# DeltaNet and a multiplicative FFN on one core: outputs without a drain, narrower corner products, and a new list of steps

## The chip, the core and the metric

The kernel runs on one core of a Trainium2 chip. A core has five engines that run side by side, each through its own queue in order: TensorE (PE, with its weight loads, PEld), VectorE (DVE), ScalarE (ACT), GpSimd (POOL), and SyncE (SP), which here only issues DMAs. TensorE multiplies a stationary block by a moving one and writes to PSUM; DVE and ACT read PSUM, POOL does not. The metric is the device time of one execution, in microseconds (us); lower is better.

## What is computed

The reference is a delta-rule attention followed by a feed-forward block. Batch 4, 8 heads, 768 tokens, head size 48; the FFN has 3072 tokens, model width 384, hidden width 1024; all in fp32.

```python
for t in range(S):
    kt, vt, bt = (k_n[:, :, t], v[:, :, t], beta[:, :, t, None])
    y[:, :, t] = np.einsum('bhd,bhde->bhe', q[:, :, t], state)
    v_old = np.einsum('bhde,bhd->bhe', state, kt)
    state = state + bt[:, :, :, None] * np.einsum('bhd,bhe->bhde', kt, vt - v_old)
...
a = x @ w1
b = x @ w2
h = a * b @ w3
return h @ w_out
```

Here `k_n` is k with each row divided by its norm, and `x` is y with the heads of a token put side by side.

## The kernel before

**Tiling.** The 768 tokens are cut into 12 chunks of 64 (`C`), and chunks are taken two at a time (`j = m // 2`), which makes 512 token rows of the FFN (`u`). A tile holds two batches (z = 0, 1) in its two halves of 64 partitions, two more (r = 0, 1) and the 8 heads along the free side. `half(z)` is partitions 64z to 64z+63, `feat(z)` the first 48 of them, `quarter(x)` partitions 32x to 32x+31.

**Steps.** Each piece of work is a Python generator that issues some instructions and yields. A list of names, `ORDER` (line 39), says in which sequence all the steps are taken; the n-th time a name stands there, the n-th step of that piece is issued. At the end `in_text_order` ties every engine's instructions to the sequence of the list. So the list sets the order in each of the five queues, and the semaphores set who waits for whom. The pieces, with m a chunk, j a pair, u an FFN block:

- `k`, `q`, `v`, `p`: loads by SP (`p` is eight DMAs a step). `P`: a piece of a weight: loads by SP into one of five `raw` buffers (four DMAs for `P24` to `P35`), two passes on ACT, two on DVE, and an add on POOL that frees the buffer.
- `d`, `K`, `Q`: k and q turned to features first. `g`, `N`, `n`: norms and scaling (`g` has squares on POOL in an `o` buffer, sums on DVE).
- `s` (`scores`, line 371): for each r, TensorE forms K·K and K·Q of all heads in a pair of PSUM banks; DVE writes `U`; then ACT copies the K·Q part to `PT` (line 405) and POOL masks it (chunks 0, 1 and 4 to 11), or DVE does both (chunks 2 and 3).
- `u`, `V`, `e`: a triangular inverse of 64x64 blocks, by 32x32 blocks. `V` is 31 pairs of small DVE instructions for two chunks; in PSUM, it holds one of the two pairs of banks meanwhile. `e` (`corner`, line 543) makes the off-diagonal corner: a 32x32 transpose on DVE (line 557), two rounds of TensorE products (line 574), with copies by ACT after each (lines 605 and 622). For pairs 0 and 1 (`TURNED`, chunks 0 to 3) the blocks are turned by copies instead of a trip through DRAM.
- `c` (`chain`): the state's chain from chunk to chunk: a product with the state, a subtraction on DVE, the product with the inverse, `X` on DVE (line 688), the product for the new state, and its sum on DVE.
- `y` (`outputs`, line 714): below. Its `xT` is the FFN's input; six small DMAs (line 779) then spread each head's last 16 features.
- `t`, `f`: W3·W_out folded. `a0`, `b` (line 872): the first FFN block. `a`, `h`, `i`, `j` (line 991): the others, by a scheme of fewer products; `G`, `W`, `S`, `T` form its sums on POOL. `o` (line 1101) and `x`: the last product and the stores, through two `o` buffers.

**PSUM.** Eight banks of 512 fp32 columns: `two_banks()` hands out two pairs in turn (`ps_w`), to scores, corners, chain, outputs and the inverse; `bank()` hands out four single ones (`ps_f`) to the rest.

**Outputs before.** For each head h and batch half z there is a state product (48 rows, from `feat(h % 2)`) and an X·PT product (64 rows, from half (z + h) % 2), which add up in PSUM. The place is `feat(h // 4)` and bank (h + z) % 2. X·PT of a bank thus comes from one half of the rows, while the state products come from the head's own half: for z = 0 the two agree, for z = 1 they don't. So all products of the first sort are issued, then TensorE is drained (`pe.drain()`), then the state products of z = 1 are issued:

```python
        for mode, todo in enumerate(modes):
            if mode:
                drain = pe.drain().ins
```

TensorE's counts in the profile are twice those of the code: each fp32 product shows as two matmuls (32 products in the code are 64 in a row of the profile).

Of the kernel before, what the change touches and what calls it, by code (L numbers as in the profile page):

```python
# [39 lines left out]
V0 P0 k0 beta P18 P13 P0 P18 P0 P0 P11 g0 P13 K0 P18 K0 P11 P18 P10 P13 P13 q0 P3 P3 P11 g0 beta  # L40
beta K0 K0 K0 k1 K1 P10 P11 P12 P3 P12 g0 g0 Q0 P10 g0 g0 g0 g0 g0 P8 Q0 Q0 Q0 K1 K1 K1 Q0 K1 P3
N0 P9 k2 P8 P8 P10 s0 P8 N0 g1 s0 s0 s0 s0 s0 s0 u0 q1 P2 Q1 P9 p2 P2 P12 P12 P9 Q1 g1 Q1 Q1 P2
u0 g1 Q1 d2 d2 u0 P5 P1 t0 t0 t5 t5 P9 t2 t2 P4 P6 s1 s1 P5 P5 P2 s1 P1 s1 s1 s1 u1 g1 P1 u1 u1
t4 V0 V0 P5 V0 V0 P4 t10 P7 P4 t3 t3 V0 V0 P1 f1 P6 P6 t4 V0 P7 V0 V0 t10 t1 P14 P7 P4 V0 f0 V0
P6 P16 P16 V0 V0 P7 t1 s0 P19 P19 P19 P19 V0 f1 P17 k3 p2 v1 V0 V0 P14 P14 P14 V0 f2 P17 f2 f0 V0
f2 P15 v0 P20 f1 t11 f0 P17 P17 f5 V0 V0 P16 t11 P16 t8 P15 V1 V0 t8 f5 t9 V0 V0 t6 P15 V0 n0 n0
f5 V0 V0 V0 V0 t9 P20 P20 V0 t6 P22 P22 P22 f4 P23 P23 V0 f4 f4 P21 P21 P15 t7 t7 V0 s1 V0 V0 V0
V0 g1 d2 d2 P22 f3 f3 P24 P20 g1 g1 p3 g1 P26 p3 P30 e0 e0 e0 t12 t14 e1 e1 g1 f3 e0 e0 d3 d3 N1
s2 s2 s2 P23 P23 t12 e0 f6 e0 p4 s2 P24 e1 e1 t14 s2 e0 P24 s2 P25 c0 P26 f7 u2 P30 P24 c0 e1 e1
P21 P21 d3 d3 y0 y0 P26 P26 P31 t15 t13 s3 s3 s3 s3 s3 s3 t13 c0 n1 n1 P32 t15 u2 u2 u3 c0 P30 f7  # L50
e1 P25 P25 P31 P31 P27 c1 c1 u3 u3 f6 e1 c1 V1 V1 V1 y0 P31 f6 f7 P25 P27 V1 V1 V1 V1 P30 b1 c1
# [5 lines left out]
d5 p5 c2 c2 y2 a04 e3 s4 N2 e3 s4 a03 s4 b6 b6 s4 s4 s4 s4 T e3 T T d5 n3 d5 a04 e3 b4 b4 b7 s5
n3 k6 g3 u4 s5 s5 s5 s5 s5 s5 b5 b7 b5 a05 T c3 c3 a06 a05 a06 u5 V2 p6 g3 a07 a07 c3 c3 g3 S0 S0
S0 V2 g3 V2 V2 N2 oD0 y3 y3 V2 V2 W oA0 S0 S0 V2 V2 S0 S0 S0 c3 v5 n5 V2 V2 S0 S0 S0 S0 V2 v4 oB0
V2 V2 V2 xA0 V2 V2 xB0 V2 V2 oA0 S0 S0 S0 n4 oB0 xA0 d6 y3 k7 xA0 V2 n4 oC0 V2 V2 V2 a10 xB0 S0  # L60
V2 V2 xC0 G1 V2 xD0 a10 a10 V2 oC0 a10 a10 d6 xC0 xC0 xC0 xD0 V2 V2 i10 V2 h10 c3 c4 V2 V2 j10 V2
V2 V2 a10 h10 i10 a12 V2 V2 h10 W W a12 p6 V2 a12 a12 j12 e4 g3 g3 h10 c4 a12 h10 a12 h12 d6 d6
# [6 lines left out]
V3 V3 V3 V3 a20 a20 i20 h20 a22 h20 g4 c5 g4 g4 g4 a22 V3 j22 d8 h20 h20 e6 i20 g4 a22 d8 a22 h22
a22 a22 i22 e6 V4 e6 c6 i20 h22 e6 i22 h22 n7 h22 e6 e6 a21 a21 a21 n6 c6 p9 c6 s8 i22 N4 h21 h22  # L70
i21 a21 s8 a21 s6 c6 y6 s8 s8 j21 s8 v8 a21 h21 i21 y6 d9 d9 e7 p9 e7 s8 s8 e7 e7 s7 h21 h21 i21
h21 a23 c6 c6 e7 a23 i23 a23 n8 n8 d9 e7 S2 N4 d9 a23 s9 s9 s9 s9 s9 n7 s9 k10 s9 u8 g5 a23 a23
c7 c7 h23 h23 i23 i23 c7 c7 g5 u9 h23 h23 V4 V4 V4 j23 h23 S2 g5 g5 V4 V4 V4 V4 p10 v9 V4 y7 y7
V4 V4 oA2 V4 V4 d10 V4 y7 V4 V4 S2 oD2 S2 d10 xA2 V4 S2 S2 oB2 oC2 V4 c7 xB2 V4 V4 V4 V4 oB2 xB2
xC2 xD2 p10 V4 V4 V4 oA2 V4 V4 a30 a30 G3 a30 a30 S2 S2 oC2 k11 V4 xC2 j30 s9 V4 xD2 xC2 V4 V4 V4
V4 V4 V4 xA2 xA2 xC2 g5 a30 h30 a30 i30 a32 h30 V4 V4 V4 e8 h30 i30 c7 a32 j32 h30 h30 g5 a32 a32
i32 g5 g5 d10 d10 i30 a32 a32 e8 h32 h32 i32 p11 e8 e8 a31 a31 c8 e8 s8 c8 g5 a31 j31 e8 c8 n9 c8
h32 h32 h32 y8 y8 c8 e9 e9 i31 d11 d11 h31 e9 e9 n9 a31 c8 s10 a31 p11 i32 N5 s10 s10 a31 h31 s10
s10 s10 s10 c9 c9 h31 e9 e9 d11 d11 u10 i31 i31 s11 a33 a33 S3 a33 v11 h31 h31 s11 s11 s11 s11
s11 a33 c9 i33 a33 a33 c9 h33 h33 s11 u11 i33 i33 j33 h33 h33 V5 V5 V5 V5 y9 S3 h33 V5 V5 V5 v10  # L80
n10 n10 oA3 S3 S3 V5 V5 oD3 V5 oB3 s10 y9 y9 oC3 V5 V5 S3 S3 V5 V5 V5 V5 V5 xA3 xB3 V5 V5 n11 V5
V5 oB3 V5 xB3 xD3 xC3 xC3 xD3 oA3 G4 a40 S3 S3 a40 a40 V5 oC3 N5 V5 V5 V5 xA3 a40 a40 xC3 h40 a40
h40 i40 V5 V5 V5 V5 h40 h40 V5 j40 h40 i40 V5 V5 V5 V5 a42 a42 a42 a42 i42 h42 a42 j42 xA3 V5 V5
a42 i40 h42 i42 h42 h42 a41 a41 a41 a41 h41 a41 V5 e10 e10 e10 e10 h42 n11 a41 i42 h41 i41 i41
i41 h41 e10 e11 h41 e10 c9 j41 a43 a43 a43 S4 c9 e11 e11 e11 h41 c10 c10 h43 c10 a43 e11 j43 xC3
a43 c10 a43 i43 h43 i43 i43 h43 h43 e11 h43 c10 c10 y10 y10 c11 s11 oD4 c11 c11 c11 oA4 xA4 y11
S4 S4 S4 oB4 oA4 y11 y11 S4 S4 S4 xA4 xB4 oB4 xB4 oC4 xC4 xA4 a50 xC4 S4 oC4 xC4 xD4 xD4 a50 G5
a50 h50 a50 a50 i50 a50 h50 i50 i50 h50 h50 j50 h50 a52 a52 a52 a52 i52 a52 a52 h52 a51 h52 i52
j52 h52 h52 h52 i51 a51 a51 a51 h51 i52 S5 a51 a51 h51 i51 j51 h51 h51 i51 a53 a53 a53 a53 h53
a53 a53 h53 j53 h51 h53 h53 h53 i53 i53 i53 xC4 o5 x5 o5 S5 S5 o5 o5 x5 S5 S5 S5 S5 o5 x5 x5 o5  # L90
x5 x5 x5 x5 x5 x5 S5 o5 x5 x5 x5 x5
# [1199 lines left out]
```

## Time and profile before

| | |
|---|---|
| time, median of 3 runs | 556.02 us (555.83 to 556.4) |
| time of the profiled execution | 556.05 us |
| its span, first to last instruction | 554.0 us |
| granted TensorE clock, mean | 0.997 |
| scores, TensorE, K·K and K·Q at once (line 381) | x384, mean 287 ns |
| scores, TensorE, 64 columns (line 387) | x768, mean 228 ns |
| outputs, X·PT (line 747) | x768, mean 216 ns |
| outputs, state (line 747) | x704, mean 221 ns |
| xT copies, ACT, 48x256 (line 768) | x96, mean 366 ns, 30.5 us in all |
| mask, POOL, 128x512 (line 407) | x20, mean 1285 ns |
| X, DVE, 128x768 (line 688) | x12, mean 953 ns |

The page gives each engine's busy time in 40 slices of the span (13.85 us each); a digit is tenths, 9 is 90% or more:

```profile
PE   3577999999999999999999999999999999999997
PEld 2464666688788988889988889988899888998897
DVE  4989998899877878659977579858587654123332
ACT  4788388855543112332022530123231121300000
POOL 8575554633658970455343355510492212342141
PEclk9998999999999999999999999999999999999999
```

Matmuls overlap one another, so a row's mean duration is longer than what one costs in a run; the distance from the start of one group to the start of the next says what a group takes. In a row of a group, the last columns are busy time, mean duration, and idle time of the engine just before, with what ended it. In a row of the timeline they are start and duration in us, engine, line, operation, tiles, shape and count, and in brackets the idle time before and what ended it.

### The profile page before, as it was taken

What the parts mean: (1) busy time and instruction counts of PE and PEld (TensorE: products, weight loads), DVE (VectorE), ACT (ScalarE), POOL (GpSimd) and SP (SyncE); (2) the same over time, 40 slices, a digit from 0 to 9 for tenths busy, and PEclk for the clock granted to TensorE, in tenths of its full rate; (3) what the DMA queues carried; (4) which work ended last, traced back from release to release, by engine and by line L of the source; (5) the groups of instructions that cost most, each with busy time, mean ns of one, the idle gap of its engine ahead of it and who ended that gap; (6) DMA issues with size and microseconds to landing.
All of it is one profiled execution on the core that took longest, in us unless ns stands there. A gap on an engine that the chain in (4) does not pass through costs nothing.

```text
span 554.0 us, 19883 instructions
## 1 busy us (share of the span) xinstructions
PE 522.9 (94%) x8540; PEld 448.4 (81%) x8540; DVE 389.2 (70%) x850; ACT 188.4 (34%) x393; POOL 257.7 (47%) x278
## 2 busy tenths in 40 slices
PE   3577999999999999999999999999999999999997
PEld 2464666688788988889988889988899888998897
DVE  4989998899877878659977579858587654123332
ACT  4788388855543112332022530123231121300000
POOL 8575554633658970455343355510492212342141
PEclk9998999999999999999999999999999999999999
DMA  8976986579457345345553564253601220020001
GB/s 254 213 199 193 208 184 134 130 154 142 61 82 128 74 110 86 57 96 92 100 109 63 80 121 85 83 81 46 124 15 44 62 52 2 10 66 1 0 1 57
DMA packets 197687, 52.64 MB, mean 95 GB/s; under 512 B 185344, under 2 KB 191488, under 8 KB 197600
## 3 DMA queue, kind: packets, MB, share of 16 engines
q1 hardware_dynamic: 193408, 50.59, 44.8%
q10 hardware_dynamic: 4192, 0.79, 1.0%
q8 instruction: 67, 1.10, 0.8%
q14 instruction: 20, 0.16, 0.1%
HBM read 41.25 MB, written 8.91 MB: 91 GB/s over the span
## 4 chain that ended last, share of the span: by engine, by line
PE 77%; DVE 6%; ACT 6%; DMA 5%; SPq 3%; issue 1%; POOL 1%; ACTq 0%; POOLq 0%; DVEq 0%
PE ps_f L991 33%; PE ps_f L1101 19%; PE ps_f L872 7%; PE ps_w L648 5%; PE ps_w L747 4%; PE ps_w L574 3%; PE ps_w L387 2%; PE ps_w L381 2%; DMA raw<-in_moe_w_dram 1%; DMA ktok<-in_k_dram 1%; SPq L251 1%; ACT columns L444 1%; DVE w L804 1%; ACT KQ L360 1%; DVE tb L482 1%
## 5 line engine op out<-in xcount | busy, mean ns | idle before, releaser
L999 DVE TENSOR_TENSOR ab<-ab,ps_f 128x512 f32<-128x512 f32 x80 | 54.6, 683 | 58.4 <-PE ps_f L991 57.8
L1072 POOL TENSOR_TENSOR ab<-ab 128x512 f32<-128x512 f32 (+1 forms) x56 | 61.3, 1119 | 42.7 <-PE ps_f L1101 25.9
L991 PE MATMUL ps_f<-xT,w1s 128*128 128x256 f32 x320 | 78.5, 382 | 0.0
L1038 POOL TENSOR_TENSOR ab<-ab,late 128x512 f32<-128x512 f32 x19 | 24.1, 1271 | 107.8 <-DVE ab L999 106.3
L991 PEld LDWEIGHTS ps_f<-xT,w1s 128*128 128x128 f32 x320 | 59.9, 190 | 7.9
L1101 PE MATMUL ps_f<-w,ab 128*128 128x192 f32 x376 | 65.5, 328 | 0.0
L1101 PEld LDWEIGHTS ps_f<-w,ab 128*128 128x128 f32 x376 | 61.3, 190 | 1.3 <-issue 0.7
L852 PE MATMUL ps_f<-w2s,w3T 128*128 128x384 f32 x128 | 45.3, 505 | 4.9 <-POOL w2s L808 4.9
L407 POOL TENSOR_TENSOR PT<-PT,smask 128x512 f32<-128x512 f32 x20 | 25.7, 1285 | 50.8 <-ACT PT L405 50.8
L1101 PE MATMUL ps_f<-room,ab 128*128 128x192 f32 x272 | 47.2, 328 | 0.0
L498 DVE TENSOR_TENSOR ps_w<-ps_w,tb 128x31 f32<-128x31 f32 (+15 forms) x124 | 43.3, 349 | 4.2
L768 ACT COPY xT<-ps_w 48x256 f32<-48x256 f32 x96 | 30.5, 366 | 44.5 <-PE ps_w L747 44.0
L1101 PEld LDWEIGHTS ps_f<-room,ab 128*128 128x128 f32 x272 | 44.3, 190 | 0.6 <-issue 0.3
L493 DVE TENSOR_TENSOR tb<-ps_w,Ub 128x31 f32<-128x31 f32 (+15 forms) x124 | 42.0, 338 | 3.6 <-ACT ps_w L473 0.3
L1007 ACT COPY ab<-ps_f 128x512 f32<-128x512 f32 x20 | 11.7, 586 | 95.0 <-PE ps_f L991 89.3
L991 PE MATMUL ps_f<-xT,room 128*128 128x256 f32 x160 | 41.3, 385 | 0.2 <-DVE ab L999 0.2
L852 PEld LDWEIGHTS ps_f<-w2s,w3T 128*128 128x128 f32 x128 | 24.0, 195 | 20.5 <-POOL w2s L808 5.5
L991 PE MATMUL ps_f<-xT,w2s 128*128 128x256 f32 x160 | 40.1, 381 | 0.0
L991 PE MATMUL ps_f<-x_room,w2s 128*128 128x256 f32 x160 | 38.9, 386 | 0.0
L991 PEld LDWEIGHTS ps_f<-xT,room 128*128 128x128 f32 x160 | 29.5, 190 | 5.4 <-DVE ab L999 1.0
L991 PEld LDWEIGHTS ps_f<-x_room,w2s 128*128 128x128 f32 x160 | 29.5, 190 | 5.2 <-DVE late L999 1.0
L808 POOL TENSOR_TENSOR w<-w,raw 128x512 uint32<-128x512 uint32 x16 | 21.9, 1373 | 24.9 <-DVE w L804 9.1
(146 smaller groups left out, 1022.0 us busy)
## 6 DMA issues: line engine op xcount, KB each, us to landing
raw<-in_moe_w_dram SPq DMA_DIRECT2D x16, 512.0 KB, 5.5
vtok<-in_v_dram SPq DMA_DIRECT2D x24, 192.0 KB, 4.3
raw<-in_moe_w_dram SPq DMA_DIRECT2D x24, 192.0 KB, 4.2
out_dram<-osb SPq DMA_DIRECT2D x46, 96.0 KB, 1.7
ktok<-in_k_dram SPq DMA_DIRECT2D x44, 96.0 KB, 3.4
raw<-in_moe_w_out_dram SPq DMA_DIRECT2D x8, 384.0 KB, 4.6
perm<-in_k_dram SPq DMA_DIRECT2D x40, 64.0 KB, 2.8
perm<-in_q_dram SPq DMA_DIRECT2D x32, 64.0 KB, 2.5
```

The source lines that it names most:

```text
L407: pool.tensor_tensor(out=PT, in0=PT, in1=smask[:].unsqueeze(1).to_broadcast([P, H, C]), op=ALU.mult)
L493: dve.tensor_tensor(out=tv, in0=V[:, 0 : s + 1, s : s + 1].to_broadcast([P, s + 1, n]), in1=U[:, s, s + 1 : BS].unsqueeze(1).to_broadcast( ...
L498: dve.tensor_tensor(out=o, in0=o, in1=tv, op=ALU.subtract)
L648: pe.matmul(out(ps, r, h, z), lhsT=lhs(r, h, z), rhs=rhs(r, h, z), start=True, stop=True,)
L768: act.copy(out=xT[f, p:NP:2, b : b + NR, cc, :].rearrange("p a r t -> p r a t"), in_=pyv[f, z, b : b + NR],)
L852: pe.matmul(ps[:, 0:DM], lhsT=w3Ts[jc, kc // 4][:, kc % 4 * P : kc % 4 * P + P], rhs=wo[:, kc], start=(kc == 0), stop=(kc == KF - 1),)
L872: pe.matmul(ps[:].rearrange("p b c t -> p b (c t)"), lhsT=w[:, m, js], rhs=x[:, m, :, c0:c1].rearrange("p b c t -> p b (c t)"), start=(m = ...
L991: pe.matmul(acc[name][:, n * i : n * i + n], lhsT=ws[b][:, P * i : P * i + P], rhs=xs[x], start=new and k == 0 and i == 0, stop=k == len(t ...
L999: dve.tensor_tensor(out=o_, in0=x, in1=acc[name], op=ALU.add)
L1038: eng.tensor_tensor(out=Z1, in0=Z1, in1=late, op=ALU.mult)
L1072: pool.tensor_tensor(out=o_, in0=x_, in1=y_, op=op)
L1101: pe.matmul(ps[b][:, b, :], lhsT=block(u, HF * f + i, z)[:, P * b : P * b + P], rhs=ws_[w][:, i], start=first and i == 0 and (b == 0 or n ...
```

## The change

Three parts.

1. For chunks 1 and 4 to 11 (`SWAPPED`) outputs keep every product of a head in that head's own half of the rows (h % 2), and the PSUM bank is h % 2. For that, `scores` writes K·K and K·Q of an odd head side by side, as it did for even ones (one product of 128 columns for two of 64); the copy to `PT` becomes four copies of 64x256, two of them from one half of the partitions to the other; and a new step of `outputs` copies half of `X` to the other half (`Xc`, two ACT copies of 64x384, in an `o` buffer). The drain and its order are left out there, and xT is copied in four parts of 48x512 in place of eight of 48x256. Chunks 0, 2 and 3 stay as they were.
2. The first corner product of turned blocks (chunks 0 to 3) has 33 stationary columns instead of 64; its result lands in the first quarter of each half, and ACT's copy moves it to the second.
3. `ORDER` is new from beginning to end; the nine chunks' `y` have one more step each.

The diff, with the list cut to the lines that are spoken of:

```diff
 ORDER = """
...
-s2 s2 s2 P23 P23 t12 e0 f6 e0 p4 s2 P24 e1 e1 t14 s2 e0 P24 s2 P25 c0 P26 f7 u2 P30 P24 c0 e1 e1
-P21 P21 d3 d3 y0 y0 P26 P26 P31 t15 t13 s3 s3 s3 s3 s3 s3 t13 c0 n1 n1 P32 t15 u2 u2 u3 c0 P30 f7
...
-N1 b1 v2 P32 V1 V1 P27 V1 s1 y1 y1 b2 V1 d4 V1 V1 P28 P29 P32 b2 P27 V2 V1 V1 V1 y1 b3 V1 V1 P28
...
-a43 c10 a43 i43 h43 i43 i43 h43 h43 e11 h43 c10 c10 y10 y10 c11 s11 oD4 c11 c11 c11 oA4 xA4 y11
...
+d3 e1 y0 y0 p4 P25 P30 P26 P24 P24 P31 t15 t13 t13 s3 s3 s3 s3 s3 s3 P26 c0 t15 c0 N1 u3 u3 P32
...
+P27 y0 P25 b1 P27 P32 b3 V1 y1 y1 P31 P27 V1 b0 V1 V1 V1 d4 v2 b1 b1 b3 V1 y1 P28 P29 P28 b1 b2
...
+d7 d7 h11 a13 a13 e5 e5 h11 s7 s7 s7 s7 s7 s7 a13 a13 h11 u7 s6 s6 s7 u6 c5 h13 a13 a13 h13 s6
...
+c11 e11 y10 y10 oD4 c11 c11 y11 oA4 y11 S4 y11 S4 xA4 oB4 xB4 y11 S4 oA4 S4 S4 oB4 xB4 oC4 xA4
...
 """
...
+    SWAPPED = (1, *range(4, NCH))
...
-                    if h % 2 == 0:
+                    if h % 2 == 0 or m in SWAPPED:
                         pe.matmul(
-                            ps[half(z), 0, n : n + 128], lhsT=x[:, 0, :],
+                            ps[half(z), h % 2, n : n + 128], lhsT=x[:, 0, :],
                             rhs=x.rearrange("p j t -> p (j t)"), start=True, stop=True,
                         )
...
-                act.copy(out=by_parity(PT), in_=psv[:, :, :, 1, :])
+                if m in SWAPPED:
+                    for z in range(2):
+                        for e in range(2):
+                            act.copy(
+                                out=PT[half(e), NP * z : NP * z + NP, :],
+                                in_=psv[half(z), :, e, 1, :],
+                            )
+                else:
+                    act.copy(out=by_parity(PT), in_=psv[:, :, :, 1, :])
...
-            ps = products(
-                lambda n, z: (U[rows(z), C * n : C * n + C], z ^ n % 2),
-                lambda n, z: T11[rows(z), BS * n : BS * n + BS],
-                half,
-            )
         else:
             L = T11
-            ps = products(
-                lambda n, z: (U[rows(z), C * n + BS : C * n + C + 1], z ^ n % 2),
-                lambda n, z: T11[rows(z), BS * n : BS * n + BS],
-            )
+        ps = products(
+            lambda n, z: (U[rows(z), C * n + BS : C * n + C + 1], z ^ n % 2),
+            lambda n, z: T11[rows(z), BS * n : BS * n + BS],
+        )
         yield
         for z in range(2):
-            x = quarter(2 * z + turned)
             act.copy(
-                out=by_parity_of(L[x, 0:N].rearrange("p (g t) -> p g t", t=BS)), in_=ps[x]
+                out=by_parity_of(
+                    L[quarter(2 * z + turned), 0:N].rearrange("p (g t) -> p g t", t=BS)
+                ),
+                in_=ps[quarter(2 * z)],
             )
...
+        swapped = c in SWAPPED
+        if swapped:
+            Xc = in_turn(ffn, [P, NR * NP, D], "o", 2, "Xc")
+            for e in range(2):
+                act.copy(
+                    out=Xc[half(e)].rearrange("p (r a) d -> p r a d", r=NR),
+                    in_=X[half(1 - e)].rearrange("p r (a e) d -> p r a e d", e=2)[:, :, :, e],
+                )
+            yield
...
-            return pyv[feat(h // NP), (h + z) % 2, NR * z + r, h % NP // 2, :]
+            return pyv[feat(h // NP), (h if swapped else h + z) % 2, NR * z + r, h % NP // 2, :]
...
-        for mode, todo in enumerate(modes):
+        for mode in range(2):
+            todo = modes[0 if swapped else mode]
...
-            for r in range(NR if mode == 0 else 0):
+            for r in range(NR if mode == 0 and swapped else 0):
+                for a in range(0, NP, 2):
+                    for z in range(2):
+                        for h in (a, a + 1, NP + a, NP + a + 1):
+                            x = half(h % 2)
+                            todo.append((
+                                h, z, r, Xc[x, NP * r + h // 2, :] if z else X[x, r, h, :],
+                                PT[x, r, NP * z + h // 2, :],
+                            ))
+            for r in range(NR if mode == 0 and not swapped else 0):
...
-            if mode:
+            if mode and todo:
                 drain = pe.drain().ins
...
-        for i in issued[0]:
+        for i in issued[0] if issued[1] else ():
             in_order(i, drain)
...
-        for z in range(2):
+        for e in range(2):
+            f = feat(e)
+            for p in range(2 if swapped else 0):
+                act.copy(
+                    out=xT[f, p:NP:2, :, cc, :].rearrange("p a b t -> p b a t"), in_=pyv[f, p]
+                )
+        for z in range(0 if swapped else 2):
             for e in range(2):
                 f = feat(e)
```

More of the change, by code (lines that the diff above doesn't have):

```diff
@@ L57 @@
[L57 to L62, printed above, removed]
@@ L69 @@
[L69 to L74, printed above, removed]
@@ L87 @@
[L87 to L91, printed above, removed]
+V0 P0 k0 beta P18 P13 P0 P18 P0 g0 P11 beta beta P0 P10 q0 P3 k1 K0 P13 P18 K0 K0 P18 P11 K0 Q0
@@ new lines @@
+t9 P15 V0 V0 V0 V0 n0 P15 V0 t9 V0 V0 f5 n0 f5 P20 P20 t7 g1 V0 V0 f4 g1 P22 f4 P20 f4 V0 V0 t12
+t12 P24 p3 P22 V1 P22 t7 f3 f3 V0 d2 d2 e0 e0 e0 d3 e0 g1 P21 d3 f3 t14 e0 P26 s2 e0 e0 N1 s2 s2
+p3 P30 P24 e1 e1 P23 P23 P23 e0 f6 n1 t14 s2 s2 s2 n1 e1 c0 c0 u2 P26 f7 e1 e1 P21 P21 u2 u2 d3
+d3 e1 y0 y0 p4 P25 P30 P26 P24 P24 P31 t15 t13 t13 s3 s3 s3 s3 s3 s3 P26 c0 t15 c0 N1 u3 u3 P32
+P25 P25 P31 u3 f7 P31 P30 P30 f7 e1 e1 s1 c1 V1 V1 V1 c1 V1 V1 V1 V1 f6 f6 P32 P32 V1 c1 c1 V1 V1
+P27 y0 P25 b1 P27 P32 b3 V1 y1 y1 P31 P27 V1 b0 V1 V1 V1 d4 v2 b1 b1 b3 V1 y1 P28 P29 P28 b1 b2
@@ new lines @@
+n2 y1 b0 b0 V1 c1 P27 P28 P28 P35 V1 b2 b2 b0 V1 b2 V1 V2 P29 P29 a03 V1 a00 V1 d4 V1 V1 V1 P29
+a03 a01 a02 a02 P33 P34 V1 V1 V1 a01 a00 k4 g2 a06 a06 V1 V1 V1 V1 V1 b7 b7 V1 a07 a07 P35 a04
+a04 a05 V1 a05 c1 a02 a02 e2 g2 e2 g2 k5 b3 b3 p4 v3 b5 g2 e2 e2 a01 d4 d4 p5 c2 n2 c2 g2 P33 g2
+b4 b4 e2 a00 b5 P35 a01 e2 e2 b6 a00 e2 b6 e3 P33 c2 c2 e3 a03 P34 P34 g2 g2 g2 P33 P34 e3 P35 y2
+b4 d5 d5 c2 a03 y2 e3 e3 e3 c2 T b6 p5 k6 a04 s4 N2 s4 s4 s4 s4 T b4 b7 g3 s4 s4 d5 n3 e3 e3 d5
+s5 n3 s5 s5 s5 s5 s5 b6 s5 a04 a07 a07 g3 g3 c3 u4 u5 S0 V2 c3 a06 c3 g3 V2 p6 b5 b7 a05 V2 N2 c3
@@ new lines @@
+d7 d7 h11 a13 a13 e5 e5 h11 s7 s7 s7 s7 s7 s7 a13 a13 h11 u7 s6 s6 s7 u6 c5 h13 a13 a13 h13 s6
+i13 s5 j13 V3 V3 c5 p8 g4 v6 h13 y5 g4 g4 i13 i13 S1 h13 h13 V3 V3 V3 y5 n6 V3 y5 y5 V3 V3 V3 V3
+V3 V3 d8 oC1 V3 V3 V3 oA1 S1 S1 c5 xA1 oA1 oD1 xA1 S1 S1 v7 S1 S1 V3 V3 V3 oB1 d8 s6 G2 V3 V3 V3
+a20 xB1 oB1 V3 V3 V3 a20 V3 j20 xB1 xA1 k9 xC1 oC1 V3 V3 xD1 V3 V3 V3 a20 a20 p8 xC1 xC1 h20 V3
+V3 a20 xD1 V3 V3 xC1 a20 h20 i20 i20 a22 V3 V3 h20 V3 N3 h20 h20 a22 j22 e6 g4 g4 c5 a22 a22 i22
+g4 g4 a22 g4 d8 d8 h22 a22 e6 e6 e6 i20 h22 i22 c6 a21 n6 e6 c6 N4 e6 h22 h22 c6 a21 p9 s8 s8 s8
```

67 lines of the change are left out of this document (35 added, 32 removed).

## The prediction

> **What bounds the kernel now.** I read the page's totals and slices first, then the chain that ended last, then busy time by stretch of the span, then TensorE's order of time around one outputs step and one score step, then the groups split by shape.
>
> ```profile
> span 554.0 us, 19883 instructions
> PE 522.9 (94%) x8540; PEld 448.4 (81%) x8540; DVE 389.2 (70%) x850; ACT 188.4 (34%) x393; POOL 257.7 (47%) x278
> ...
> PE 77%; DVE 6%; ACT 6%; DMA 5%; SPq 3%; issue 1%; POOL 1%; ACTq 0%; POOLq 0%; DVEq 0%
> ...
> 40.00:60.00 20.00, 15.13 (x45) 8.73 (x45) 18.69 (x46) 14.16 (x26) 11.35 (x10) 0.91 0.71 179
> 100.00:120.00 20.00, 19.15 (x434) 14.38 (x433) 18.84 (x44) 16.58 (x35) 9.84 (x10) 1.00 0.60 127
> 300.00:400.00 100.00, 99.62 (x2032) 87.72 (x2031) 72.45 (x151) 25.80 (x60) 37.64 (x36) 1.00 0.48 88
> ```
>
> The last three lines are stretches: length, then busy time of PE, PEld, DVE, ACT and POOL. To about 110 us loads, DVE and ACT set the pace (DVE 18.7 to 18.8 of 20 us, PE short of full); from there PE is full at full clock, and ACT has three quarters of its time free. Behind 141 us a microsecond of TensorE work is a microsecond of the kernel; ahead of it only if DVE's chain allows. I therefore price steps as TensorE slots: from the first matmul of a group to the first of the next.
>
> ```profile
> 401.14 0.66 PE L747 MATMUL ps_w<-KQ,S 48*48 48x64 f32 x32
> 401.62 1.07 PE L747 MATMUL ps_w<-PT,X 64*48 64x64 f32 x64
> 402.81 0.66 PE L747 MATMUL ps_w<-KQ,S 48*48 48x64 f32 x32
> 403.41 2.87 PE L1101 MATMUL ps_f<-w,ab 128*128 128x192 f32 x16
> ...
> 109.81 0.67 PE L872 MATMUL ps_f<-xT,w1s 128*128 128x256 f32 x2 [0.73 <-DMA xT<-xT]
> ...
> L405 ACT COPY PT<-ps_w 128x512 f32<-128x512 f32 x20 | 11.7, 586 | 24.8 <-DVE U L393 24.8
> L1138 ACT COPY osb<-ps_f 128x384 f32<-128x384 f32 x6 | 2.9, 479 | 21.4 <-PE ps_f L1101 13.6 <-DVE ps_w L498 7.0 <-DVE tb L493 0.8
> L574 PE MATMUL ps_w<-T,U 33*33 33x32 f32 x512 | 6.1, 195 | 0.0
> L574 PE MATMUL ps_w<-T,U 33*64 33x32 f32 x256 | 4.5, 220 | 0.4 <-ACT xT L768 0.3
> ```
>
> In the outputs of chunk 9 (first lines) the last 32 state products start 1.19 us after the 64 X·PT products; 64 such instructions stream in 2 x 0.48 = 0.96 us. The other 0.23 us is the drain. The 109.81 line is the last place where a load holds PE in the front.
>
> **The drains.** After the change the 128 instructions run on: 0.48 + 0.96 + 0.48 us, and 0.12 for the turn to 128-wide products (402.81 to 403.41 is 0.60, less 0.48), 2.04 in place of 2.27. Bounds of the saving per chunk: 0 (the hand-over is needed all the same) and 0.33 (2.27 less two 64-instruction slots of 0.97, the chain product at 366.47 to 367.44). I take 0.23, by the row at hand. Chunks 4 to 11 lie in the full part: 8 x 0.23 = **-1.84**. Chunk 1's (at 110 us) I count as nothing: DVE's chain to the corner of chunk 2 covers it; bound -0.33.
>
> **Scores.** In nine chunks the odd heads' two 64-column products become one of 128: 32 instructions in place of 48 per group. Even heads' pairs start every 0.107 us already (381.46, 381.57, 381.68), the time that 128 columns stream, beside the odd ones in the other row half. So the slot (0.92 to 1.10) stays: **0**, bounds ±0.05 for each of 18 groups, ±0.9.
>
> **ACT's copies.** PT takes four copies of 64x256 for one: xT's 48x256 copies go at 2.59/8 = 0.32 us each back to back, so 1.35 for 0.59, +0.76 us per group. Xc adds two copies of 64x384 (479 ns for 128x384): +0.96. xT takes four of 48x512 (2.36 us for four in a row, L360 at 33.68) for eight (2.59): -0.2. ACT gains 2 x 0.76 + 0.96 - 0.2 = 2.3 us a chunk, 20 us in all; with 25.8 of 100 us busy this is no load. What counts is who waits. Behind PT's copies and Xc on ACT's in-order queue stand evictions of FFN banks (L1007, 586 ns, with PE work of 1 us or more to spare); POOL's mask follows, but outputs come 57 us or more of PE work after their scores, so it hides. The ps_w pair is freed 0.76 later, after DVE's 0.69 (U) and both hand-overs some 2.3 us after the group. In the new list chunk 5's first score group needs the pair 1.9 us of PE work after chunk 4's last, and the first c5 step after the s7/s6 run about 1.9: 0.4 each. Xc needs X (0.95, L688), then 0.96, and 0.3 of hand-overs: 2.2 us after the product of c. Between that product and the outputs the new list has 1.75 us for chunk 4, 2.6 for 1, 8 and 11, and 3.5 or more elsewhere: 0.45 for chunk 4. Sum **+1.25**; bounds 0 (the PE is late already) and +2.6 (chunks 1, 8 and 11 late by 0.45 each too, as DVE's in-order queue holds X back). Xc shares the two `o` buffers with POOL's squares and the stores; where they follow each other, over 8 us of PE work lie between, or the earlier user is long done: 0.
>
> **Corners of chunks 0 to 3.** 33 stationary columns for 64: slot 0.68 (364.72 to 365.40) for 0.95 (141.34 to 142.29), 0.27 each. Chunks 2 and 3 (141 and 154 us): **-0.54**; chunks 0 and 1 (81, 92 us) nothing, since the wait at 109.81 comes behind them; without that cover -0.54 more. ACT's two evictions (578 ns) only change quarter.
>
> The row for such matmuls is 0.68 us for 64, 10.6 ns from start to start. [...]
>
> **The list.** It moves nearly every step by a few places; queue by queue:
> - SP: loads keep their order to chunk 4. P32 takes the raw buffer that P24 frees, and P24's DVE and POOL passes now stand behind P26's. On DVE P24 ends about where P26's ended (95.98), its POOL add (1.29) at 97.3; P32's issue came at 92.57 + 8 x 0.6 = 97.4. Just in time: 0. Later on, V4's load and stores swap places behind stores already due.
> - DVE and ACT in the front: one PT group of chunk 1 stands before V0's copies into PSUM, +0.76, and the T transpose of chunk 0 has 0.7 more ahead of it. Corner 0 starts on that transpose's heel (80.56 + 0.72, PE at 81.32), so PE loses about 0.8 there, which the wait at 109.81 swallows: 0, or +0.8 without that cover.
> - The corner of chunk 2: PE came at 141.34, its transpose ended at 140.89, so 0.45 spare. The new list has 1.0 us more DVE work before the transpose and 0.5 us less PE work: up to +0.5 + (1.0 - 0.45) = 1.05; I take +0.5.
> - Later waits that the list loosens: between the two products of corner 2 stand 1.3 us for 1.03 (it waited 0.35), an o step comes between y10 and c11 (0.34 lost there), and i22 stands where h22 waited for its bank (a22's slot at 283.01 is 1.32 where 0.86 is usual; 0.3 of it counted). 0.27 + 0.34 + 0.3: -0.9.
> - POOL keeps its adds, in another order; 38 to 40 of 100 us busy in the full part: 0.
> List: **-0.4**, bounds -2 (slots after 140 us are 3.2 us over the usual for their kind; 1.2 of it, at e3 and s7, stands in the new list as before) and +2 (as much again the other way).
>
> **Sum**: -1.84 - 0.54 + 1.25 - 0.4 = -1.53. The profiled run took 556.05 (554.0 of span, 2.05 around it), 0.03 over the median 556.02: **554.5 us**. About 0.2% (1.1 us, 554.9 to 557.1) is what can be told from no change here.
>
> **Rivals.**
> 1. *The gap stays.* Drain or not, the array empties between groups of other shape (48 rows of state, 64 of X·PT). For it: 0.12 us at each turn to 128-wide products. Against: 401.62, where that same change of shape costs nothing. [...] Price: 1.84 back, 556.05 - 0.54 + 1.25 - 0.4 = 556.4, no change. 15%.
> 2. *Slower: SP's queue in the front.* If P24 frees its buffer late, P32's four issues wait, and P27, y0's six xT moves (which end the wait at 109.81), v2, P28, P29 and y1's six wait with them; DVE is in order, so V1 stops behind a late P piece, and corner 2 is late by the same. For it: SP issues back to back from 92.57 to 106.8, POOL already waits 3.4 us for xT. Against: my 97.3 against 97.4. It turns the sign from 1.53 us late on and shows from 2.6 us on; P24 three microseconds late gives 554.5 + 3.0 = 557.5. 19%.
> 3. *The list does more.* Waits after 140 us fall as far as the bound: -2 for -0.4, so 552.9, or 552.4 with the corners of chunks 0 and 1 on the path. 11%.
>
> **Chances.** Forecast 55%, own range 553.3 to 555.9 (the waits on ACT's copies at their bounds). Faster: 0.44 of the forecast and 0.11 of rival 3, **0.55**; within 0.2%: 0.11 of the forecast and 0.15 of rival 1, **0.26**; slower: rival 2, **0.19**. Range 552.0 to 557.6: rival 3 with the scores' lower bound of -0.9 reaches to 551.5 (half of that kept), rival 2 ends at 557.5.
>
> **What would show it.** Right: 128 L747-type matmuls as one run of about 2.04 us in chunks 4 to 11; the turned corner's slot at 0.68; score slots unchanged at 0.92 to 1.10; ACT some 20 us busier; PE's waits naming the PT and Xc copies summing to about 1.25. Wrong: a hole of 0.2 us left in the outputs; score groups over 1.1; PE waiting longer than 1 us for xT or for chunk 2's corner, which would be rival 2.

## The result, and the profile after

The changed kernel takes **564.43 us** (median of 4 runs, 563.68 to 564.92), beside 556.21 us for the kernel before on the same chip: a ratio of **1.0138**, interval 1.0119 to 1.0158. It is 8 us slower. The forecast was 554.5, with a range to 557.6. The profiled execution of the changed kernel took 563.68 us, 561.8 of them span. The times of the experiments are medians; two of them include one execution in a slow state (588.91 us of the old list with all new code, 580.39 us of the kernel before with 64 products more), which the ratios leave out.

From the page of the changed kernel, its totals, the chain that ended last, and three rows of the 40 slices:

```profile
span 561.8 us, 19368 instructions
PE 520.2 (93%) x8252; PEld 444.6 (79%) x8252; DVE 390.0 (69%) x850; ACT 209.8 (37%) x429; POOL 255.8 (46%) x278
...
PE 73%; DMA 8%; DVE 7%; ACT 5%; SPq 4%; issue 2%; POOL 0%; DVEq 0%; ACTq 0%
```

```profile
PE   2464998999999999999999999999999999999997
...
DVE  3688996899976898748987569876688645114422
...
PEclk9997998999999999999999999999999999999999
```

TensorE is busy 2.7 us less than before, in a span 7.8 us longer, and its share of the chain fell from 77% to 73%. The slices show where: the first three read 246 where 357 stood, and PEclk has a 7 in the fourth slice and an 8 in the seventh. From the eighth slice (98 us) on PE reads 9, as before. The parts of the change that were to save time behind that point did so. The outputs of chunk 9 in the timeline of TensorE:

```profile
410.26 0.67 PE L777 MATMUL ps_w<-KQ,S 48*48 48x64 f32 x32
410.75 0.29 PE L777 MATMUL ps_w<-PT,X 64*48 64x64 f32 x8
...
411.64 0.63 PE L777 MATMUL ps_w<-KQ,S 48*48 48x64 f32 x32
412.20 2.06 PE L1137 MATMUL ps_f<-w,ab 128*128 128x192 f32 x11
```

The products are one run of 412.20 - 410.26 = 1.94 us, where 2.27 stood, and the second state group follows without a hole. To place the loss, the table gives when TensorE starts the same work in both profiles (us from the start of the span).

| TensorE starts | before | after | later by |
|---|---|---|---|
| first corner product of chunk 0 (step `e0`) | 81.32 | 87.58 | 6.3 |
| chunk 2's second score group (`s2`) | 87.37 | 96.10 | 8.7 |
| chunk 1's outputs (`y1`) | 110.41 | 120.48 | 10.1 |
| chunk 2's corner (`e2`) | 141.34 | 150.35 | 9.0 |
| chunk 9's outputs (`y9`) | 401.14 | 410.26 | 9.1 |
| last group of `o5` | 547.38 | 555.22 | 7.8 |

**The first 6.3 us show as idle time of DVE.** Corner 0 follows DVE's T transpose, and that follows V0's last transpose (77.08 before, 83.16 after). These are stretches up to it, with busy time of PE, PEld, DVE, ACT and POOL, first of the kernel before, then of the changed one:

```profile
0.00:25.00 25.00, 9.94 (x211) 8.10 (x213) 16.77 (x29) 13.30 (x24) 20.29 (x34) 1.00 0.97 244
25.00:45.00 20.00, 13.30 (x280) 11.25 (x277) 17.68 (x31) 18.29 (x34) 14.35 (x12) 1.00 0.66 163
45.00:77.08 32.08, 31.91 (x109) 19.22 (x110) 29.99 (x81) 20.01 (x39) 17.11 (x17) 0.95 0.91 220
sum 77.08, PE 55.15 PEld 38.57 DVE 64.44 ACT 51.60 POOL 51.75; mean PE 18.38 PEld 12.86 DVE 21.48 ACT 17.20 POOL 17.25
```

```profile
0.00:25.00 25.00, 7.54 (x182) 6.65 (x186) 12.23 (x19) 11.61 (x19) 18.01 (x33) 1.00 0.96 225
25.00:45.00 20.00, 13.29 (x281) 11.42 (x273) 16.27 (x35) 17.12 (x33) 12.06 (x11) 1.00 0.80 178
45.00:83.16 38.16, 32.24 (x112) 19.80 (x113) 35.41 (x88) 23.23 (x47) 19.59 (x20) 0.91 0.82 194
sum 83.16, PE 53.07 PEld 37.87 DVE 63.91 ACT 51.95 POOL 49.65; mean PE 17.69 PEld 12.62 DVE 21.30 ACT 17.32 POOL 16.55
```

DVE has 64 us of work ahead of that transpose in both (64.44 and 63.91). It stands idle 77.08 - 64.44 = 12.6 us before and 83.16 - 63.91 = 19.2 us after. Of the 6.6 more, 4.5 lie in the first 25 us (25 less 16.77, against 25 less 12.23). There the new list puts g0's square ahead of P0's add on POOL, and q0's load ahead of P11's passes on ACT's queue. P0's add and one of ACT's passes in the kernel before, then the same add, q0's load and the later pass in the changed kernel:

```profile
9.15 1.01 POOL L808 TENSOR_TENSOR w2s<-w2s,raw 128x384 uint32<-128x384 uint32 x1
```

```profile
10.68 0.68 ACT L800 ACTIVATE w<-raw 128x512 f32<-128x512 f32 x1 [0.98 <-DMA raw<-in_moe_w_dram]
```

```profile
10.51 1.00 POOL L844 TENSOR_TENSOR w2s<-w2s,raw 128x384 uint32<-128x384 uint32 x1
```

```profile
7.96 0.60 ACTq L234 DMA_DIRECT2D X<-in_q_dram  x1
...
11.90 0.67 ACT L836 ACTIVATE w<-raw 128x512 f32<-128x512 f32 x1 [2.72 <-DMA raw<-in_moe_w_dram]
```

P0's add starts at 10.51 (9.15 before) and frees the buffer that SP's next issues wait for (11.54 in place of 10.19). q0's load starts at 7.96 in place of 12.08, while the DMA engines are full (share 0.96). ACT then waits 2.72 us for a weight piece where it waited 0.98, and DVE waits for ACT. These rows show the order of events; which of the moved steps costs how much was not tried one by one.

**The next 2.4 us are a stop inside TensorE and a slower clock.** From the chain that ended last, in order of time:

```profile
89.94 0.51 PE ps_w L586 x35
90.45 1.02 issue
91.47 0.66 PE ps_w L586 x29
92.14 4.04 PE ps_f L888 x8
```

The second corner product stops for 1.02 us after 35 of 64 instructions, with nothing awaited. Then f6's eight long products take 4.04 us, where they take 2.78 in the chain of the kernel before: from 91.23 to 94.64 the granted clock is 0.50. The stretch from 92 to 94 us, with the clock behind POOL's busy time:

```profile
92.00:94.00 2.00, 2.00 (x11) 1.18 (x5) 1.82 (x4) 1.95 (x5) 0.00 (x0) 0.50 0.82 228
```

The last 1.4 us, up to `y1`, hold a wait for ACT's xT copies (0.85 at 104.68, where the kernel before waits 0.50) and the waits for X (0.42) and Xc (0.21). From `y1` to the end the changed kernel gains 10.07 - 7.84 = 2.2.

### The profile page after: what moved, and what is told of

It reads as the page before. It is cut to its first block, busy times and chain, and to the rows that moved or that the text cites. A ratio compares the mean times of both kernels' runs of the same rounds, so it can differ in the third digit from the quotient of the medians.

```text
span 561.8 us, 19368 instructions
## 1 busy us (share of the span) xinstructions
PE 520.2 (93%) x8252; PEld 444.6 (79%) x8252; DVE 390.0 (69%) x850; ACT 209.8 (37%) x429; POOL 255.8 (46%) x278
## 3 DMA queue, kind: packets, MB, share of 16 engines
q8 instruction: 65, 1.06, 0.8%
## 4 chain that ended last, share of the span: by engine, by line
PE 73%; DMA 8%; DVE 7%; ACT 5%; SPq 4%; issue 2%; POOL 0%; DVEq 0%; ACTq 0%
PE ps_f L1027 33%; PE ps_f L1137 19%; PE ps_f L908 6%; PE ps_w L657 5%; PE ps_w L777 3%; DMA raw<-in_moe_w_dram 2%; PE ps_w L586 2%; DMA X<-in_q_dram 2%; DVE tb L494 2%; PE ps_w L385 2%; DVE ps_w L499 2%; DMA raw<-in_moe_w_out_dram 1%; ACT columns L456 1%; ACT PT L412 1%; DMA Ub<-Ud 1%
## 5 line engine op out<-in xcount | busy, mean ns | idle before, releaser
L283 POOL TENSOR_TENSOR sq<-ktok 128x384 f32<-128x384 f32 x24 | 20.8, 871 | 47.4 <-DMA ktok<-in_k_dram 29.6
L412 ACT COPY PT<-ps_w 64x256 f32<-64x256 f32 x72 | 26.4, 366 | 25.4 <-DVE U L397 24.6
```

The lines of the kernel that those rows point to most:

```text
L412: act.copy(out=PT[half(e), NP * z : NP * z + NP, :], in_=psv[half(z), :, e, 1, :],)
```

## The experiments

A ratio is to the kernel before, in runs on the same chip beside it. "Late" is against the profile of the kernel before. Products of TensorE are numbered as the trace shows them, from the first of the kernel.

**List or code.** The old list with all new code, and the new list with the old code. The lists' edits, shortened:

```diff
 ORDER = """
...
-c1 N1 b1 v2 P32 V1 V1 P27 V1 s1 y1 y1 b2
+c1 y1 N1 b1 v2 P32 V1 V1 P27 V1 s1 b2 y1 y1
...
-c4 y4 y4 c4 e5 d7 d7 h11 c4
+c4 y4 c4 e5 d7 d7 h11 y4 y4 c4
...
```

> The changed kernel's code (no drain, 33 columns, four PT copies, Xc, 128-column scores) with the list of the kernel before; the nine new steps (Xc) stand right behind the X step of their chunk, and the outputs of chunks 1, 4, 6 and 8 are moved back by one or two TensorE groups so that X and Xc fit in front of them. Theory 'the list lost it': the code parts are worth what I summed, -1.84 - 0.54 + 1.25 = -1.1 against 556.2, so 554 to 556. Rival 'the code lost it' (four PT copies on ACT, Xc, or TensorE itself): 562 or more.

582.15 us, ratio 1.0426 (1.0339 to 1.0514): in the rival's band, which had no upper end, and slower than the change as a whole, so neither theory foresaw its size. In its profile it is 7.0 late at `y1` and then loses another 17.5.

> The code of the kernel before (drain, 64 columns, one PT copy) with the changed kernel's list, without its nine Xc steps. Theory 'the list lost it': 564.4 + 1.1 = 565.5, between 564.5 and 567. Rival 'the code lost it': 556 to 558.

567.75 us, 1.0191 (1.0150 to 1.0232), a little above the band. It is 9.0 late at `y1`, nearly as the changed kernel, and loses 3.5 more to the end, where the changed kernel wins 2.2. So the new list alone makes most of the loss in the front. Of the 3.5 behind it, 2.4 are three stops of TensorE at products 3902, 4916 and 5171 (what these are follows below), so whether the new list by itself gains there is not shown.

**Where in the list.** The new code throughout; the first 63 names, then the first 355, in the order of before:

```diff
 ORDER = """
-V0 P0 k0 beta P18 P13 P0 P18 P0 g0 P11 beta beta P0 P10 q0 P3 k1 K0 P13 P18 K0 K0 P18 P11 K0 Q0
...
+V0 P0 k0 beta P18 P13 P0 P18 P0 P0 P11 g0 P13 K0 P18 K0 P11 P18 P10 P13 P13 q0 P3 P3 P11 g0 beta
...
```

> The changed kernel, but all steps that the list of before names ahead of the first score step (63 names, the first 23 us) are taken in the order of before; everything else in the new order. Theory 'the order of the first 20 us is where it starts' (P0's add behind g0's square, q0's load ahead of its place on ACT's queue, Q0 before K1): the start of the inverse V0 comes back by 4.4 us and the end by 3 to 4, 560.5 to 561.5. Rival 'the losses between 50 and 100 us stand by themselves' (P pieces and s2 in DVE's and POOL's queues): the regained time is lost in those waits, 563 to 564.5.

562.70 us, 1.0106 (1.0069 to 1.0143). Its stretches ahead of V0's last transpose:

```profile
0.00:25.00 25.00, 9.94 (x212) 8.10 (x213) 16.69 (x29) 13.30 (x24) 20.29 (x34) 1.00 0.95 245
...
sum 81.04, PE 54.58 PEld 38.24 DVE 65.81 ACT 51.85 POOL 50.89; mean PE 18.19 PEld 12.75 DVE 21.94 ACT 17.28 POOL 16.96
```

DVE's idle time of the first 25 us is back to that of before (16.69 busy), and V0 ends 2.1 us earlier. But by `y1` this run is as late as the changed kernel (9.9): it stops at products 726, 853 and 981, for 0.67, 0.89 and 2.53 us, and has the clock halved for 3.41 us at 102.2. The first theory named the right place and too large a gain; the rival was right that it is lost again, though the profile shows it lost in these stops, and not in the queues of DVE and POOL.

> The changed kernel, but all steps that the list of before names ahead of the first step of chunk 1's outputs (355 names, about the first 110 us) are taken in the order of before, the rest in the new order. Theory 'all the loss is ahead of 110 us': 564.4 - 9.5 = 555, between 554 and 556, no worse than the old list with the new code. Rival 'the new list also loses behind 110 us': over 558.

560.26 us, 1.0058 (1.0028 to 1.0087). The time is in the rival's band, but not for its reason: with the old order it is only 1.4 late at corner 0, and 6.4 at `y1`, by stops of 1.62 and 1.55 us at products 854 and 1236 and a half-clock stretch at 92.8. From there it gains 2.2, as the changed kernel does.

**One part at a time**, on the old list: the corner alone, and chunk 1's outputs alone (`SWAPPED = ()` and `SWAPPED = (1,)`).

> The kernel before, with its own list; only the turned corners' first product is the new one with 33 columns. The old list with all new code stood 6.4 us late at chunk 1's outputs, so some part of the code costs in the front. Theory 'it is chunk 1's copies': the narrow corner is free, 555.5 to 556.3. Rival 'it is the narrow corner': 559 or more.

556.55 us, 0.9996 (0.9973 to 1.0019): the narrow corner costs nothing that can be told.

> The kernel before, with its own list and its old corner; only chunk 1 has the new outputs (128-column scores, four PT copies for one, Xc, no drain), with Xc right behind X and the outputs one FFN group later. Theory 'chunk 1's copies': 0.9 us more on ACT before the inverse's copies into PSUM at 43 us, and X plus Xc (2.2 us) in front of the outputs at 110 us, where PE has little else to do; with what a half-clock stretch of 3.4 us adds (1.7) 558.5 to 561. Rival 'chunk 1 is free': 555.7 to 556.5.

567.35 us, 1.0174 (1.0137 to 1.0211): slower by 9.7 us, far beyond the 561 that the theory allowed. The rows of TensorE that waited for nothing the profile shows include:

```profile
92.45 0.56 PE L660 MATMUL ps_w<-vtok,TT 64*64 64x48 f32 x22 [1.36 <-issue]
...
157.56 0.90 PE L660 MATMUL ps_w<-X,ktok 64*64 64x48 f32 x46 [1.36 <-issue]
```

They are products 854 and 2126, both in the middle of a group.

> The order of before up to chunk 1's outputs and the new order behind, as in the run that ended at 560.3, but chunk 1 keeps its old outputs with the drain (so chunks 4 to 11 alone are new; the corner has 33 columns). From chunk 1's outputs to the end the new list with the new code won back 2.2 us (10.07 late at chunk 1's outputs, 7.84 at the end). Theory 'chunk 1's copies cost in the front': 556.2 - 2.2 = 554.0, between 553 and 555.5, faster than both kernels. Rival 'the narrow corner or the seam between the lists costs': 558 to 560, as with chunk 1.

559.48 us, 1.0034 (1.0012 to 1.0055): not faster than before. The time is in the rival's band, though the narrow corner, one of its two causes, is cleared by the run with the corner alone. In its profile (556.99, among its fastest runs) TensorE stops at products 3520 (1.56) and 4788 (1.15).

> The code of the kernel before; its list for the first 155 names (about 52 us, past the point where TensorE takes up the fold of W3 and W_out again at 45 us), and the changed kernel's order behind, without its Xc steps. With the new list throughout the same code took 567.75. Theory 'the list's loss is made by 50 us, and TensorE, which is full from 45 to 87 us, carries it on': 567.75 - 8, so 559 to 560.5. Rival 'the order of weight pieces, corners and scores between 50 and 110 us loses as much by itself': 563 or more.

563.94 us, 1.0122 (1.0103 to 1.0141): the rival holds. Its V0 ends at 79.28, 2.2 late, and it is 5.3 late at `y1`. So the first 50 us do not hold the whole of the list's loss.

**What the stops are.** In all these profiles the stops with nothing awaited fall on the same numbers to within 4 products, whatever work stands there: 727, 854, 981, 1109, and so on by 127. The page counts instruction loads in its part on the DMA queues; for the changed kernel:

```profile
q8 instruction: 65, 1.06, 0.8%
```

The columns are loads, MB and share: 1.06 MB in 65 loads is 16 KB each, and 8252 products in 65 loads are 127 a load, which is called a block below. That is an estimate by these totals: no row says which products a load holds. Four runs test it: one moves the work against the block ends, one moves a step out of the dense stretch, one keeps the number of products, one starts V0 earlier.

> The changed kernel with one shift in its list: P1's ACT and DVE steps and the second step of N0 stand behind the four steps that start the inverse V0, not ahead of them. Theory 'the queues of ACT and DVE ahead of V0 are what makes it start 4.4 us late': 1.6 us on ACT (two passes 1.0, norms 0.6) go out of its way, corner 0 and the end come 1.5 to 2 earlier, 562.4 to 563. Rival 'the fold on TensorE, full from 52 to 87 us, sets the pace': 564 to 565.

563.72 us, 1.0132 (1.0085 to 1.0178): no gain, and between the two bands. V0's first step comes at 46.90 in place of 49.08, yet its last transpose at 84.00 in place of 83.16. Ahead of it DVE has 64.0 us of work again and is idle for 20.0, only elsewhere. The theory of the queue just ahead of V0 falls. The rival isn't shown either: from 45 us to that transpose TensorE is busy for 33.33 of 39.0 us, so it isn't full.

> The changed kernel with one step moved: the fold's f6 (eight long products, 2.8 us) stands between chunk 0's scores and the second corner product, as in the list of before, not behind the corner. In the changed kernel 64 + 96 + 64 short products follow one another there; the trace shows a stop of 1.02 us inside the second corner (product 727, 1.33 us after a 16 KB instruction load ended) and a half-clock stretch of 3.41 us behind it. Theory 'TensorE's instructions come late': both go, scores of chunk 2 start 2 to 2.7 earlier, 561.7 to 562.5. Rival 'the stop only moves to the next group': 564 to 564.8.

564.95 us, 1.0120 (1.0082 to 1.0157): the rival holds. The stop left the corner and came back in the next dense group, at product 854, with the clock halved from 96.58 on, for 6.83 us:

```profile
97.32 0.89 PE L658 MATMUL ps_w<-vtok,TT 64*64 64x48 f32 x22 [1.73 <-issue]
```

> The changed kernel with 64 tiny products more (as the profile counts them; 32 in the code, 16 columns, overwritten at once) in front of Q0, where TensorE waits 7 us for a load. They shift every later TensorE instruction by half a 16 KB block. Theory 'stops come where a block of 128 products and their weight loads ends': the stops seen at products 727, 2112 and 3748 (all 128 n plus a few) keep these numbers and so fall 64 products earlier in the work, none stays inside the second corner of chunk 0; the time changes by -2.5 to +1 by where they fall. Rival 'the corner waits for late data': the stop stays in the corner, now at product 791, and the time at 564.4.

```diff
         ps = [bank([P, NR, NP, C]) for z in range(2)]
+        for _ in range(32 if m == 0 and i else 0):
+            pe.matmul(
+                ps[0][0:32, 0, 0, 0:16], lhsT=ident[half(0), 0:32],
+                rhs=ident[half(0), 0:16], start=True, stop=True,
+            )
```

568.20 us, 1.0206 (1.0164 to 1.0249). No stop in the corner any more (neither at 727 nor at 791); the waits at 2112 and 3748, which the expectation names too, were of another kind, for POOL (0.47 us) and for ACT (0.46 us) by the changed kernel's trace. The stops are at 1109, 3520, 4534, 4788 and 7710 of all products, all on the same grid of 127, so elsewhere in the work. The last four take 5.0 us together, where the changed kernel has no such stop behind `y1`; the time is outside the band, 3.8 over the changed kernel.

> The kernel of before with the new outputs for chunk 1 alone (it took 567.35 where 557.6 was taken by the kernel before), with one 64-column product more for each odd head in chunk 1's scores (it writes the same values again), so that TensorE has as many products as before and every later one has its old place in its 16 KB block. Theory 'the old list suffers since block ends move into dense groups': 558 to 561, the four PT copies and Xc alone. Rival 'chunk 1's copies cost it all': 566 to 568.

```diff
                             rhs=x.rearrange("p j t -> p (j t)"), start=True, stop=True,
                         )
+                        if h % 2:
+                            pe.matmul(
+                                ps[half(z), 1, n + C : n + 128], lhsT=x[:, 0, :],
+                                rhs=x[:, 1, :], start=True, stop=True,
+                            )
```

558.83 us, 1.0027 (0.9999 to 1.0056), where the same edit without these products took 1.0174. Thirty-two products more, of no use, make it 8 us faster. What they change is the place of every later product between the block ends: it is that of the kernel before again.

**How much block ends can do.**

> The old list with all of the new code, as in the run that took 582.15, but with a 64-column product more for each odd head in the scores of the nine chunks (it writes the same values again), so that TensorE has the 8540 products of before and each has its old place in its 16 KB block. Theory 'block ends': the 26 us go, 555 to 562. Rival 'the copies on ACT stand badly in the old list': 575 to 582.

575.18 us, 1.0292 (1.0255 to 1.0329): inside the rival's band. Its waits of TensorE name the new code's copies where the old list leaves no time for them:

```profile
233.76 1.15 PE L663 MATMUL ps_w<-S,KQ 48*64 48x48 f32 x64 [2.35 <-DVE S L725]
...
318.68 1.13 PE L592 MATMUL ps_w<-T,U 33*33 33x32 f32 x64 [4.09 <-ACT PT L418]
```

The first stands where I moved chunk 4's outputs; the second is the pair of banks held by the four PT copies, which stand behind chunk 6's xT copies on ACT. The added products are not free either (see the last pair: by its figures some 8 us for the 18 groups of the nine chunks, an estimate), so how much of the 26 us was block ends stays open.

> The kernel before, its own list and code, with 64 tiny products more (32 in the code, 16 columns, overwritten at once) in front of Q0, where TensorE stands idle. Theory 'block ends': every later block ends 64 products earlier in the work, and the old list, in which only 0.4 us of stops inside groups are seen, gets stops it did not have: 559 to 568. Rival 'the block ends only matter where a group is short of cover anyway': 556 to 557.5.

572.43 us, 1.0253 (1.0201 to 1.0305), beyond the band: the kernel before, slower by 14 us through 64 tiny products. They did not stand in an idle stretch here, as was expected: in this order TensorE has Q0's data by then, and the 64 take 3.59 us of its time (from 21.66). In the profile, at 577.32 one of the slower runs, the first scores start 4.6 late, in part by this. From there to the end it loses 16.7 more, with eight stops of half a microsecond or more and nothing awaited, 10.0 us together, and three half-clock stretches of 3.41 us, two of them in a row. Two of the stops:

```profile
121.12 0.21 PE L752 MATMUL ps_w<-KQ,S 48*48 48x64 f32 x1 [2.33 <-issue]
...
244.65 0.66 PE L579 MATMUL ps_w<-T,U 33*33 33x32 f32 x27 [1.76 <-issue]
```

> The changed kernel with 32 tiny products more in front of Q0 (64 more took 568.2, none 564.4). Theory 'block ends': another time again, anywhere from 561 to 570, with stops at 727 + 127 n in the count of all products. Rival 'the 568.2 came from the 64 products' own time in the front': half of it, 566.3, stops where they were.

563.74 us, 1.0098 (1.0067 to 1.0130).

> The changed kernel with 96 tiny products more in front of Q0. Theory 'block ends': 561 to 570, not in order of the number added. Rival 'the products' own time': 564.4 + 1.5 x 3.8 = 570.

565.45 us, 1.0133 (1.0094 to 1.0172). With 0, 32, 64 and 96 products more the ratios are 1.0138, 1.0098, 1.0206 and 1.0133: not in order of the number added, so it is not the products' own time, which here fell where TensorE waits for q. The intervals of 0, 32 and 96 overlap; that of 64 lies above them, but for a touch with that of 96. All of them are slow: block ends spread the new list over 1.1%, but none of these places takes its loss in the front away.

Two of the profiles divide that loss: the one with 32 products more, and the one of the new list with the old code. Between 60 us and `y1`, TensorE in neither of them stands still for 0.3 us or more with nothing awaited, or runs at half clock. With 32 products more it is 6.3 us late at corner 0, 6.1 at `s2` and 7.8 at `y1` (118.19); with the old code 7.3 at corner 0 and 9.0 at `y1` (119.45). So by these profiles the new list makes 7.8 of the changed kernel's 10.1 us at `y1` without any stop, and the stop with the slower clock behind it the other 2.3. The end time does not show that gain, since the run with 32 more has 2.8 us of stops behind `y1`.

> The old order to chunk 1's outputs, the new order behind, new outputs for chunks 4 to 11 alone, corner with 33 columns, and a 64-column product more for each odd head in those chunks' scores (the same values again), so that TensorE has its 8540 products. Without the added products this took 559.48 (1.0034 of before), with stops of 1.56 and 1.14 us at products 3520 and 4788. Theory 'the parts are worth what was summed': the two stops go, and with them the gain of 2.2 us behind chunk 1's outputs shows: 0.995 to 0.999 of before. Rival 'the new tail needs its own places': 1.002 to 1.006.

564.71 us, 1.0131 (1.0092 to 1.0170).

> As the run before it, with chunk 1 new as well. Without the added products it took 560.26 (1.0058 of before), 6.4 late at chunk 1's outputs by stops at 854 and 1236 and a half-clock stretch. Theory 'block ends': these go, chunk 1's outputs come 2 to 4 late (its copies, as where chunk 1 alone was new), 0.998 to 1.003. Rival: 1.006 or more.

565.79 us, 1.0147 (1.0110 to 1.0184). Both theories of the pair fall on something I had overlooked. The products of a score group of these chunks take 1.49 us in the mean with the added ones, where they took 1.02; over the 16 groups of chunks 4 to 11 that is 7.5 us, and the first run is 5.4 (0.97%) slower than the same kernel without them. So this pair says nothing of the tail's block ends. No version found here beats the kernel before.

## Why the prediction was wrong, point by point

- **The bound** was read right in the main: to 110 us DVE and its loads set the pace. 64 us of DVE work stand ahead of V0's last transpose in both kernels, and what changes is DVE's idle time. The rows at 40 and 100 us hid, though, that TensorE is as full from 45 to 77 us (31.91 of 32.08 us, DVE 29.99).
- **The drains.** Right in mechanism, under-sized: 1.94 us for 2.04 predicted, so 0.33 a chunk, the far bound that I gave. Rival 1 (a gap that stays) did not come: the second state group starts 411.64 - 410.75 = 0.89 us after the first of the 64 X·PT products, for 0.96 by the rows of before.
- **Scores.** Right: a slot is 0.92 to 1.07 where nothing is awaited. **Corners.** Right: 0.68 and 0.69 us in chunks 2 and 3. 64 products in 0.68 us are 10.6 ns each.
- **ACT's copies.** Busy time rose by 209.8 - 188.4 = 21.4 us, for 20 predicted. Behind 141 us TensorE's waits that name PT come to 0.8 + 0.4 = 1.2 us, for a sum of 1.25; Xc cost 0.21, in chunk 1. The new list leaves more room for them: with the old one the same copies held TensorE for 4.09 us at one place.
- **Everything behind `y1`** was forecast at -1.5 and gave -2.2. Luck has a part in that: no stop fell there in the changed kernel's profile, while nearly the same tail has two of 1.56 and 1.15 us where chunk 1 kept its old outputs.
- **The list** is the term that failed: "-0.4, bounds -2 and +2", where by the two profiles above it lost some 8 to 9 us by `y1`. Two of its steps were false. "DVE and ACT in the front" counted the orders around V0's copies and corner 0, put 0.8 us on them, and set that to nothing by the wait at 109.81 as cover; but a wait of 0.73 us can't cover the 6.3 that corner 0 came late. And "SP: loads keep their order" and "POOL keeps its adds, in another order" (at 0) passed over the first 25 us: the add that frees a buffer moved behind a square, and a load that ACT issues moved ahead of the weight pieces. There 4.5 of the 6.6 us of DVE's idle time arose. Giving back that order alone restored DVE's busy time there, but brought V0's end only 2.1 us forward, for 1.9 us more of DVE's work then stood ahead of it (65.81 for 63.91). With the old order all the way to `y1`, corner 0 came 4.8 us forward. So the steps behind the first 25 us count as well.
- **What no term held:** where TensorE's instruction blocks end, and the half clock behind a short hole (0.50 from 91.23 to 94.64). The change takes 288 products out (8540 to 8252) and so moves every block end. In the changed kernel's front that is 2.4 us between corner 0 and `s2`, and the run with 32 products more, which has neither there, is 2.3 us less late at `y1`. Rival 2 had the sign and not the mechanism: a late add on POOL (1.31 us at 101.27) does hold SP's next load in the chain after, but by then 8.7 of the 10 us were lost.

What stays open: which of the moved steps make the loss, since only whole stretches of the list were given back and every such shift also shifts stops; and what the new code would give in a list made for it with a front like the old one.

## What to carry to other kernels

Where an in-order engine is the bound, add up its work and its idle time ahead of the step that ends the stage, in both orders, from the first microsecond; don't price a reordering only near the step that it was made for. Treat a list tuned to one program as part of that program: adding or removing a few dozen TensorE instructions moved the time here by up to 2% beyond their own time, so vary their number before judging an edit. An edit that only takes products out of TensorE can lose by where the others then stand, as chunk 1's did (1.0174, and 1.0027 with the old number of products).

## What the runs showed of the hardware

**TensorE's stops with nothing awaited lie on a grid of 127 products, some 1.4 us behind an instruction load.** In the 20 profiles TensorE stands still 58 times for 0.5 us or more after 60 us with nothing awaited that the profile shows. All 58 lie within 4 products of the numbers 727 + 127 n, in kernels with quite different lists; chance would give 9 in 127 of them. Each ends 1.21 to 1.84 us (median 1.42) after a 16 KB instruction load has landed; the one at 727 in the changed kernel 1.33 us after. The waits that do name an engine or a load lie elsewhere too: at product 1424, for one, the kernel before waits 0.73 us for xT. The 58 come where short products follow one another: 64 products of a corner pass in 0.68 us (150.35 to 151.03 in the changed kernel), so 127 of them in some 1.35 us, an estimate from that row. No run shows what starts such a load.

**Half-clock stretches follow stretches in which TensorE is little busy.** Behind 60 us a granted clock of 0.50 comes in stretches of 3.41 us, or twice that, on a fixed grid, but for the one that the end of a run cuts short. TensorE's busy share in the 3.41 us ahead mostly tells when: all nine stretches with a share of 0.53 or less, out of full clock, were followed by a half-clock one, 7 of the 10 from 0.54 to 0.58, and only 3 of some 2,870 above that. In the changed kernel two gaps of 0.64 and 1.02 us, the second partly behind the stretch, came to a share of 0.58 (87.82 to 91.23), and the half clock that followed (91.23 to 94.64) cost 4.04 - 2.78 = 1.26 us. Ahead of 60 us the share alone does not tell: in the kernel before, 0.51 (38.43 to 41.84) was followed by full clock. Why the clock falls is not shown.

**A single run varies too.** The kernel with the narrow corner alone ran from 555.03 to 561.71 us; its profiled run, at 560.14, has two half-clock stretches behind 60 us that the profile of the kernel before has not. That they make up its distance from the median of 556.55 is not shown.
